# First tokens in pairs with V first, zeros on TensorE, another queue for the maxima and score tiles in fixed turn, in a fused attention and gated MLP block

## The chip, the cores and the metric

The kernel runs on one core of a Trainium2 chip. The metric is the device time of one execution in microseconds (us). The engines are called as in the profile: PE (TensorE, matrix products; PEld is its weight load), DVE (VectorE), ACT (ScalarE), POOL (GpSimd) and SP (SyncE, which issues DMA transfers). A suffix q stands for an engine's queue, where it waits or issues.

## The reference

One layer norm feeds two branches, and the results and the input are added.

```python
xn = _layernorm(x)                                   # x: 1 x 2048 x 512
qkv = (xn @ wqkv) ...                                # 32 heads of 16
p = softmax(einsum("bhqd,bhkd->bhqk", q, k) * 16 ** -0.5)
attn = einsum("bhqk,bhkd->bhqd", p, v) ... @ wo
z = gelu(xn @ w_in);  z1, z2 = halves of z           # 896 wide each
g = einsum("ts,bsf->btf", w_sp, layernorm(z2)) + b_sp
out = x + attn + (z1 * g) @ w_out
```

Everything is float32.

## The kernel before, in words

Products are made in three parts: each operand is split into a high part (a rounded copy) and a low part (the rest), and `mm3` (L161) adds high by high, low by high and high by low into one PSUM bank. `split` (L157) does this for a PSUM tile: ACT copies the high part, DVE subtracts.

**The first stage** (L816 to L854) makes normed tokens, q and k of the first eight heads, and all of V. Tokens come in four groups of 512, each of four tiles of 128. `load_x` (L223) brings two tiles a transfer. `norm_x` (L233) takes statistics on DVE, a square root on ACT, two small DVE operations, and scales the tiles on ACT. `turn_x` (L255) turns a group with 16 PE transposes, four for each block of 128 channels, splits each block and stores it for later stages through GpSimd's queue. A block takes a PSUM tile from `spsum` (L153), of which there are three of two banks. `begin` (L168) loads a weight block in full and, with `early`, loads it a second time through GpSimd's queue straight into the rounded high part; `end` (L182) then subtracts on DVE, or, without `early`, GpSimd does both steps. `qk_group` (L287) makes q and k of a group, 24 products; `v_tile` (L334) makes V of 128 tokens, 12 products, and ACT empties the bank. The order on PE is: group 0 turned, q and k of group 0, V tiles 0 and 1, group 1 turned, V tiles 2 and 3, q and k of group 1, and so on. `load_stacks` (L598) reads q and k back from DRAM into stacks with the rows laid out for the score products.

**The attention loop** (L943 to L1014) goes over 16 pairs of heads x 4 chunks of 512 queries x 16 tiles of 128 keys, 1024 steps, three steps in every two half steps. In a half step PE makes score tiles (`scores`, L898: tile st, two products) and, 27 steps ahead, tiles of raw scores with queries on the partitions (`max_mm`, L622: tile mx); both come from `spsum`. ACT exponentiates st into pf (`exp`, L920); DVE reduces mx to maxima (`max_red`, L632). `max_fin` (L640) ends 16 tiles of maxima in 64 places: five small DVE operations, the last a transpose (L657), then a store of 16 KB to the scratch mscr one half step later, and two half steps later four loads from it into the rows of the q stack that carry the negated maxima into the score products. `pv` (L864) multiplies pf by V into tile o. `later` (L125) puts a transfer off by so many half steps; `move` (L100) issues on SP's queue, `store` (L134) on GpSimd's in the first stage and on SP's after it.

Between these, a planner inserts steps of dense work (`queue`, L857): the rest of q and k, both halves of the MLP's input (`z2_all`, `z1_all`), the product over tokens (`spatial`), the MLP's output (`mlp_out`, L565, which loads its hidden tile and x one tile ahead) and the attention's output (`attn_out`). Engine order is the order of the code. Tiles of a pool with a tag share its buffers; a tile that reuses one waits for the last reader of the old content.

Of the kernel before, what the change touches and what calls it, by code (L numbers as in the profile page):

```python
# [16 lines left out]
P = 128  # L17
# [14 lines left out]
RING = 20  # L32
LEAD = 27
# [6 lines left out]
def fused_block(ctx, tc, x, wqkv, wo, w_in, w_spT, b_sp, w_out, out):  # L40
# [86 lines left out]

    def flush():
# [23 lines left out]

    def spsum(nm):  # L153

        return ps.tile([P, 2, 512], F32, tag="s", name=nm, bufs=3)
# [12 lines left out]
    def begin(nm, src, n, blocks=1, t=None, early=None):  # L168


        t = piece(nm) if t is None else t
        rw = t512(nm + "r") if early == "t" else big.tile([P, 512], F32, tag="raw", name=nm + "r", bufs=3)
        dst, hi = rw[:, :n], t[:, 0, :n]
        if blocks > 1:
            src = src.rearrange("(c p) f -> p c f", p=P)
            dst, hi = (v.rearrange("p (c f) -> p c f", c=blocks) for v in (dst, hi))
        move(dst, src)
        if early:
            nc.gpsimd.dma_start(hi, src)
        return t, rw, n  # L180

    def end(loaded, early=False):  # L182
        t, rw, n = loaded
        if early:
            nc.vector.tensor_sub(t[:, 1, :n], rw[:, :n], t[:, 0, :n].bitcast(F32))
        else:
            gps(0.6).tensor_copy(t[:, 0, :n], rw[:, :n])  # L187
            gps(1.3).tensor_sub(t[:, 1, :n], rw[:, :n], t[:, 0, :n].bitcast(F32))
        return t
# [33 lines left out]
    def load_x(g):  # L223
        xt = [at.tile([P, 2, D], F32, tag="pf", name=f"x{g}_{i}", bufs=PF) for i in (0, 2)]
        for i in range(len(xt)):
            k = 4 // len(xt)
            t = 4 * g + k * i
            rows = x[t * P:(t + k) * P, :]
            move(xt[i], rows if k == 1 else rows.rearrange("(a p) d -> p a d", p=P))
            for j in range(k):  # L230
                xs[g, k * i + j] = xt[i] if k == 1 else xt[i][:, j, :]

    def norm_x(g, parts=1):  # L233
# [5 lines left out]
        for a in range(parts):  # L239
            tiles = range(a * k, (a + 1) * k)  # L240
            sl = slice(a * k, (a + 1) * k)
            for i in tiles:
                st = sm.tile([P, 6], F32, tag="bst", name=f"bst{g}_{i}", bufs=4)
                nc.vector.bn_stats(st, xs[g, i])
# [4 lines left out]
            nc.vector.scalar_tensor_tensor(rs[:, 1, sl], mv[:, sl, 0], -1.0, rs[:, 0, sl], ALU.mult, ALU.mult)  # L249
            for i in tiles:  # L250
                if i % 4 == 2:
                    yield
                nc.scalar.activation(xs[g, i], xs[g, i], AF.Identity, bias=rs[:, 1, i:i + 1], scale=rs[:, 0, i:i + 1])

    def turn_x(g):  # L255
        for c in range(ND):
            pt = spsum(f"xT{g}_{c}")[:, 0, :]
            for i in range(4):
                nc.tensor.transpose(pt[:, i * P:(i + 1) * P], xs[g, i][:, c * P:(c + 1) * P], ident)
            t = piece(f"xnT{g}_{c}")  # L260
            split(t[:, 0, :], t[:, 1, :], pt, 512)
            store(xscr[g][c], t)
            xnT[g, c] = t
# [70 lines left out]
    def v_tile(t, ws):  # L334
        acc = dpsum(f"v{t}", "do"[t % 2])
        sl = slice((t % 4) * P, (t % 4 + 1) * P)
        for c in range(ND):
            xt = xnT[t // 4, c]
# [226 lines left out]
    def mlp_out():  # L565
        def load(t):
            hp = []
            for i, n in enumerate((4, 3)):
                h = piece(f"hp{t}_{i}")
                move(h[:, :, :n * P].rearrange("p a (f q) -> p a f q", q=P), hscr[t // 4][:, :, t % 4, 4 * i:4 * i + n, :])  # L570
                hp.append(h)
            xt = t512(f"xr{t}")
            move(xt, x[t * P:(t + 1) * P, :])
# [38 lines left out]
    NSTEP = NP * 64  # L612
    mstep = {}
# [26 lines left out]
    def max_fin(i):  # L640
# [18 lines left out]
        later(1, move, mscr[g % 4].rearrange("b k x -> (b k) x"), ms)  # L659
# [155 lines left out]
    with tc.manual_schedule(engines=engines):  # L815
        load_x(0)  # L816
        w0 = [begin(*qk_weights(0, a), early="t") for a in range(2)]
        load_x(1)
        ones = big.tile([P, 512], F32, tag="raw", name="ones", bufs=3)
        nc.vector.memset(ones[0:32, 0:P], 1.0)  # L820
        wv = []
        for c in range(ND):
            t = (qst, kst)[c // 2][1].rearrange("p (b a f) -> p b a f", b=2, a=2)[:, c % 2]
            wv.append(begin(f"wv{c}", wqkv[c * P:(c + 1) * P, 2 * D:3 * D], 512, t=t, early="rt"[c % 2]))
        nc.gpsimd.dma_start(cscr.rearrange("o (a b) -> (o a) b", b=P), ones[0:16, 0:P])
        nc.gpsimd.memset(vhead[:, :, :, DH:], 1.0)
        nc.gpsimd.memset(vall[:, NT * H * (DH + 1):], 0.0)
        run(norm_x(0, 2))
        load_x(2)
        w0 = [end(l, True) for l in w0]  # L830
        turn_x(0)
        load_x(3)
        init_rows(0)
        wv = [end(l, True) for l in wv]
        norm = norm_x(1, 2)
        for g in range(NG):
            for y in qk_group(0, g, w0, ("d", "o")):
                if y == 0 and g == 0:
                    next(norm, 0)
# [7 lines left out]
            for t in range(4 * g, 4 * g + 4):  # L847
# [95 lines left out]
        for half in range(-2 * LEAD // 3, 2 * (N // 3 + 4)):  # L943
# [25 lines left out]
            for n in ns[1:]:  # L969
                exp(n)  # L970
            for f in final:
# [81 lines left out]
```

## Time and profile before

| | |
|---|---|
| median of 3 runs | 1966.16 us (1964.69 to 1969.37) |
| profiled execution | 1965.23 us, its span 1963.1 us |
| mean granted clock of PE | 0.997 |
| DMA moved | 294.20 MB, mean 150 GB/s |
| busy share of PE in the first 10 us | 0.92 of 10.00 us |

In rows of the order of time, the first number is the start in us from the span's start, the second how long it took, then engine, line, operation, output<-inputs by the program's names, shapes and how many were merged. In brackets stands the idle time of the engine ahead of it and what ended it. In rows of stretches stand, for each engine, busy us and how many instructions, and at the end the granted clock of PE, the share of the DMA engines that was busy, and GB/s. In lists of waits stand the total in us, how often, and the longest.

### The profile page before, as it was taken

Reading aid. Unit: us, or ns where it says so; the run is one execution under the profiler, and the core shown is the slowest. Engines: PE = TensorE matmul, PEld = TensorE weight load, DVE = VectorE, ACT = ScalarE, POOL = GpSimd, SP = SyncE. Lnnn points to the kernel's source line nnn. Section 1 sums busy time; section 2 is a strip of 40 time slices with the busy share of each in tenths; the row PEclk is TensorE's granted clock in tenths of the full one; section 3 lists DMA queues with packets and bytes.
Section 4 is the critical chain, followed back from the end, with each engine's and each line's share of the span. In section 5 each row is a group of like instructions: output and inputs, shape, how many; then the busy total and the mean of one; then the engine's idle time right before and its main releaser. Section 6 shows DMA issues by size and latency. Waiting matters only on the chain.

```text
span 1963.1 us, 32545 instructions
## 1 busy us (share of the span) xinstructions
PE 1933.9 (99%) x12544; PEld 1047.0 (53%) x12544; DVE 1372.9 (70%) x1562; ACT 1231.7 (63%) x1402; POOL 720.9 (37%) x787
## 2 busy tenths in 40 slices
PE   7999999999999999999999999999999999999998
PEld 6765555555555555555555555555555555555543
DVE  5256777777777677777777777777777777777872
ACT  4336778888777665656666665665566655556664
POOL 2234368789776931026122531017112300002100
PEclk9999999999999999999999999999999999999999
DMA  9586444363535645365545744346364645355323
GB/s 327 204 292 200 139 107 122 108 176 111 154 117 159 187 123 140 91 162 159 151 138 154 211 129 125 108 126 204 105 163 135 176 142 145 106 152 154 105 73 113
DMA packets 234195, 294.20 MB, mean 150 GB/s; under 512 B 34536, under 2 KB 134520, under 8 KB 231160
## 3 DMA queue, kind: packets, MB, share of 16 engines
q1 hardware_dynamic: 229816, 282.08, 49.4%
q0 software_dynamic: 4224, 10.04, 1.4%
q8 instruction: 99, 1.62, 0.3%
q14 instruction: 56, 0.46, 0.1%
HBM read 190.09 MB, written 101.97 MB: 149 GB/s over the span
## 4 chain that ended last, share of the span: by engine, by line
PE 91%; DVE 3%; POOL 2%; DMA 2%; ACT 1%; issue 1%; SPq 0%; DVEq 0%; POOLq 0%; ACTq 0%
PE o L877 23%; PE mx L630 15%; PE st L903 15%; PE sp L162 7%; PE sp L164 5%; PE sp L163 5%; PE mo L162 2%; PE z1p L162 2%; PE qk L162 1%; DVE mm L638 1%; PE mo L163 1%; PE mo L164 1%; PE z2p L162 1%; PE z1p L164 1%; PE z1p L163 1%; PE qk L163 1%
## 5 line engine op out<-in xcount | busy, mean ns | idle before, releaser
L638 DVE TENSOR_REDUCE mm<-mx 128x2 f32<-128x1024 f32 x1024 | 1221.5, 1222 | 501.3 <-PE mx L630 497.2
L57 ACT ACTIVATE pf<-st 128x1024 f32<-128x1024 f32 x1024 | 1028.7, 1025 | 621.9 <-PE st L903 597.2
L877 PE MATMUL o<-pf,vall 128*32 128x512 f32 (+1 forms) x5120 | 511.0, 513 | 0.0
L630 PE MATMUL mx<-kst,qst 48*128 48x512 f32 x2048 | 446.9, 434 | 3.1 <-DVE mm L638 2.0
L903 PE MATMUL st<-qst,kst 50*128 50x512 f32 x2048 | 445.6, 432 | 1.5 <-DVE mm L638 1.4
L630 PEld LDWEIGHTS mx<-kst,qst 48*128 48x128 f32 x2048 | 192.0, 185 | 268.7 <-ACT pf L57 168.6
L903 PEld LDWEIGHTS st<-qst,kst 50*128 50x128 f32 x2048 | 193.3, 185 | 164.0 <-issue 85.7
L877 PEld LDWEIGHTS o<-pf,vall 128*32 128x32 f32 x5120 | 131.4, 109 | 233.7 <-issue 211.7
L162 PE MATMUL sp<-wsp,zs 128*128 128x512 f32 x448 | 193.8, 433 | 0.3 <-DVE z1i L549 0.2
L556 POOL TENSOR_TENSOR z1i<-z1i,hhl 128x512 f32<-128x512 f32 x28 | 36.0, 1286 | 425.9 <-DVE z1i L549 422.4
L164 PE MATMUL sp<-wsp,zs 128*128 128x512 f32 x448 | 175.9, 393 | 0.0
L163 PE MATMUL sp<-wsp,zs 128*128 128x512 f32 x448 | 175.9, 393 | 0.0
L162 PEld LDWEIGHTS sp<-wsp,zs 128*128 128x128 f32 x448 | 83.9, 187 | 68.9 <-issue 52.1
L164 PEld LDWEIGHTS sp<-wsp,zs 128*128 128x128 f32 x448 | 84.1, 188 | 19.3
L163 PEld LDWEIGHTS sp<-wsp,zs 128*128 128x128 f32 x448 | 84.4, 188 | 12.2
L187 POOL CAST wo<-wo0r 128x512 fp32r<-128x512 f32 x1 | 0.6, 611 | 191.4 <-DMA wo0r<-in_wo 191.4
L310 POOL TENSOR_TENSOR qkhl<-qr,qkhl 128x512 fp32r<-128x512 f32 x24 | 30.9, 1289 | 78.9 <-ACT qkhl L57 78.8
L162 PE MATMUL z2p<-w,xt 128*128 128x448 f32 x128 | 51.3, 401 | 0.0
L162 PE MATMUL mo<-wout,hp 128*128 128x512 f32 x112 | 48.5, 433 | 0.6 <-DVE xr L593 0.4
L691 POOL TENSOR_TENSOR ob<-ob 128x512 f32<-128x512 f32 (+1 forms) x16 | 20.6, 1288 | 77.0 <-DMA ob<-rscr 54.5
L164 PE MATMUL z2p<-w,xt 128*128 128x448 f32 x128 | 46.9, 366 | 0.0
L163 PE MATMUL z2p<-w,xt 128*128 128x448 f32 x128 | 46.8, 365 | 0.0
(378 smaller groups left out, 1974.8 us busy)
## 6 DMA issues: line engine op xcount, KB each, us to landing
zs<-z2scr SPq DMA_DIRECT2D x112, 512.0 KB
escr<-e SPq DMA_DIRECT2D x60, 256.0 KB
hscr<-hhl SPq DMA_DIRECT2D x28, 512.0 KB
qst<-qscr SPq DMA_DIRECT2D x30, 384.0 KB
kst<-kscr SPq DMA_DIRECT2D x30, 384.0 KB
xscr<-xnT POOLq DMA_DIRECT2D x16, 512.0 KB, 6.0
qscr<-qkhl SPq DMA_DIRECT2D x16, 512.0 KB
kscr<-qkhl SPq DMA_DIRECT2D x16, 512.0 KB
```

What stands on the lines that cost most here:

```text
L57: return nc.scalar.activation(out, in_, func, **kw)
L162: nc.tensor.matmul(acc, lh, rh, start=first, stop=False)
L163: nc.tensor.matmul(acc, ll, rh, start=False, stop=False)
L164: nc.tensor.matmul(acc, lh, rl, start=False, stop=last)
L187: gps(0.6).tensor_copy(t[:, 0, :n], rw[:, :n])
L310: gps(1.3).tensor_sub(hl[:, 1, :], src, hl[:, 0, :].bitcast(F32))
L556: gps(1.3).tensor_add(z1, z1, hl[:, 1, :].bitcast(F32))
L630: nc.tensor.matmul(acc[:, j, :], qst[p % 2][rows, tt * P:(tt + 1) * P], kst[p % 2][rows, kc * 512:(kc + 1) * 512], start=True, stop=True)
L638: dve(1024).tensor_reduce(mmax[i // 16][:, :, t, kc], mstep.pop(i), AX.X, ALU.max)
L691: gps(1.3).tensor_mul(both[rows, 0, :], both[rows, 0, :], both[rows, 2, :])
L877: nc.tensor.matmul(acc[cols:cols + VW, a:a + w], vpack(kt - 1 + r, 2 * p + j), pf[:, j * 512 + a:j * 512 + a + w], start=(kt == 1 and a == ...
L903: nc.tensor.matmul(st[:, j, :], kst[p % 2][rows, kt * P:(kt + 1) * P], qst[p % 2][rows, c * 512:(c + 1) * 512], start=True, stop=True)
```

## The change

- **First stage.** Group 0's tiles are loaded one by one: two, then V's four weight blocks, then the other two, then the weights of q and k, then groups 1 and 2. All early loads go through SP's queue; the second loads through GpSimd's are gone. GpSimd casts V's high parts; DVE subtracts three of the low parts and GpSimd the fourth; GpSimd makes both parts of the q and k weights. Group 0 is normed and turned in pairs of tiles: the first pair, V tiles 0 and 1, the second pair, V tiles 2 and 3, then q; group 1 is turned between q and k of group 0. Group 1 is normed in pairs too, between V tiles 2 and 3.
- `turn_x` takes three PSUM tiles of two banks at once, makes all transposes, and then splits.
- 15 products of zeros (`WARM`) stand first on PE. Their operand is set by DVE. A square root on ACT stands first there.
- `spsum` gives the three tiles strictly in turn.
- The store of maxima leaves SP's queue for ACT's: it is kept in `behind` and issued behind the exponentials of a half step.
- In `mlp_out` the loads for all tiles but the first are put off by 1, 2 and 3 half steps.

```diff
@@ spsum
-        return ps.tile([P, 2, 512], F32, tag="s", name=nm, bufs=3)
+        turns[0] += 1
+        return ps.tile([P, 2, 512], F32, tag=f"s{turns[0] % 3}", name=nm, bufs=1)
@@ begin, end
-        if early:
-            nc.gpsimd.dma_start(hi, src)
...
-    def end(loaded, early=False):
+    def end(loaded, low=None, high=False):
         t, rw, n = loaded
-        if early:
-            nc.vector.tensor_sub(t[:, 1, :n], rw[:, :n], t[:, 0, :n].bitcast(F32))
+        if high:
+            low.tensor_sub(t[:, 1, :n], rw[:, :n], t[:, 0, :n].bitcast(F32))
...
@@ turn_x
+    def turn_x(g, lo=0, hi=4):
+        tiles = [spsum(f"xT{g}_{lo}_{c}") for c in range(3)]
+        sl = slice(lo * P, hi * P)
+        for c in range(ND):
+            for i in range(lo, hi):
+                nc.tensor.transpose(tiles[c % 3][:, c // 3, i * P:(i + 1) * P], xs[g, i][:, c * P:(c + 1) * P], ident)
+        for c in range(ND):
+            if lo == 0:
+                xnT[g, c] = piece(f"xnT{g}_{c}")
+            t = xnT[g, c]
+            split(t[:, 0, sl], t[:, 1, sl], tiles[c % 3][:, c // 3, sl], (hi - lo) * P)
+            if hi == 4:
+                store(xscr[g][c], t)
@@ mlp_out
-                move(h[:, :, :n * P]..., hscr[...])
+                (later if t else soon)(i + 1, move, h[:, :, :n * P]..., hscr[...])
...
-            move(xt, x[t * P:(t + 1) * P, :])
+            (later if t else soon)(3, move, xt, x[t * P:(t + 1) * P, :])
@@ max_fin and the loop
-        later(1, move, mscr[g % 4].rearrange("b k x -> (b k) x"), ms)
+        behind.append((now[0] + 1, mscr[g % 4].rearrange("b k x -> (b k) x"), ms))
...
             for n in ns[1:]:
                 exp(n)
+            while behind and behind[0][0] <= half:
+                nc.scalar.dma_start(*behind.pop(0)[1:])
@@ first stage
+        nc.scalar.activation(mhalf, epst, AF.Sqrt)
+        idle = piece("idle")
+        nc.vector.memset(idle.bitcast(F32)[:, 0, :], 0.0)
+        nc.vector.memset(mhalf, -0.5)
+        rest = dpsum("idle", "o")
+        for _ in range(WARM):
+            nc.tensor.matmul(rest, idle[:, 0, 0:P], idle[:, 0, :], start=True, stop=True)
...
+        for t, rw, n in wv:
+            nc.gpsimd.tensor_copy(t[:, 0, :], rw)
+        norm = norm_x(0, 2)
+        next(norm)
+        next(norm)
+        wv = [end(l, (nc.vector, nc.gpsimd)[c == 3], True) for c, l in enumerate(wv)]
+        turn_x(0, 0, 2)
+        next(norm)
...
+        w0 = [end(l) for l in w0]
+        run(norm)
+        v_tile(0, wv)
+        v_tile(1, wv)
+        turn_x(0, 2, 4)
+        norm1 = norm_x(1, 2)
+        next(norm1)
+        v_tile(2, wv)
+        next(norm1)
+        next(norm1)
+        v_tile(3, wv)
+        run(norm1)
```

More of the change, by code (lines that the diff above doesn't have):

```diff
@@ L32 @@
 RING = 20
+WARM = 15
 LEAD = 27
@@ L126, in later, with soon @@
         late.append((now[0] + k, fn, args))
+    def soon(k, fn, *args):
+        fn(*args)
     def flush():
@@ L337, in v_tile @@
         for c in range(ND):
+            if c == 2 and mid:
+                mid(t + 1)
             xt = xnT[t // 4, c]
@@ L612, in fused_block @@
     NSTEP = NP * 64
+    behind = []
     mstep = {}
@@ L815, in fused_block @@
     with tc.manual_schedule(engines=engines):
[L816 to L820, printed above, removed]
+        nc.scalar.activation(mhalf, epst, AF.Sqrt)
[5 more added lines that the diff above has]
+            nc.tensor.matmul(rest, idle[:, 0, 0:P], idle[:, 0, :], start=True, stop=True)
+        first = load_x(0)
+        next(first)
+        next(first)
         wv = []
@@ L824, in fused_block @@
             wv.append(begin(f"wv{c}", wqkv[c * P:(c + 1) * P, 2 * D:3 * D], 512, t=t, early="rt"[c % 2]))
+        run(first)
+        w0 = [begin(*qk_weights(0, a), early="t") for a in range(2)]
+        run(load_x(1))
+        run(load_x(2))
+        ones = big.tile([P, 512], F32, tag="raw", name="ones", bufs=3)
+        nc.vector.memset(ones[0:32, 0:P], 1.0)
+        for t, rw, n in wv:
[6 more added lines that the diff above has]
+        next(norm)
         nc.gpsimd.dma_start(cscr.rearrange("o (a b) -> (o a) b", b=P), ones[0:16, 0:P])
@@ L846, in fused_block @@
                     wq[1, a] = end(wq[1, a])
-            for t in range(4 * g, 4 * g + 4):
+            for t in range(4 * g, 4 * g + 4) if g else ():
                 next(norm, 0)
```

53 lines of the change are left out of this document (28 added, 25 removed).

## The prediction, made before the changed kernel ran

> **What bounds the kernel now.** I read the page first, then the stretches (busy time by window), then the order of time of the first 35 us and of 130 to 150 us, and last the idle rows of TensorE (the list of waits).
>
> ```profile
> span 1963.1 us, 32545 instructions
> PE 1933.9 (99%) x12544; PEld 1047.0 (53%) x12544; DVE 1372.9 (70%) x1562; ACT 1231.7 (63%) x1402; POOL 720.9 (37%) x787
> ```
>
> TensorE bounds the whole: busy for 1933.9 of 1963.1 us. All its idle time together is 29 us, so no change that leaves TensorE's instructions alone can gain more than 1.5%. The change leaves them alone from the first score tile on: in the two programs TensorE and VectorE have the same sequence of instructions in the attention loop. What can move is the 29 us of idle time and the time in which TensorE runs at a lower clock. About a third of the idle time lies ahead of 13.6 us:
>
> ```profile
> 0.73 0.96 SPq L101 DMA_DIRECT2D x<-in_x  x2
> 4.54 0.69 DVE L244 BATCH_NORM_STATS2 bst<-x 128x6 f32<-128x512 f32 x1 [3.46 <-DMA x<-in_x]
> 7.01 1.52 ACT L253 ACTIVATE x<-x,rs 128x512 f32<-128x512 f32 x2 [0.43 <-DVE rs L249]
> 7.92 0.45 PE L259 MATMUL xT<-ident,x 128*128 128x128 f32 x1 [7.92 <-ACT x L253]
> 9.34 1.52 ACT L253 ACTIVATE x<-x,rs 128x512 f32<-128x512 f32 x2 [0.43 <-DVE rs L249]
> 10.91 3.04 PE L259 MATMUL xT<-ident,x 128*128 128x128 f32 x13 [0.23 <-ACT x L253]
> 11.43 0.60 ACT L57 ACTIVATE xnT<-xT 128x512 fp32r<-128x512 f32 x1 [0.57 <-PE xT L259]
> 12.06 0.69 DVE L159 TENSOR_TENSOR xnT<-xT,xnT 128x512 fp32r<-128x512 f32 x1
> 13.60 0.63 PE L162 MATMUL qk<-xnT,wqk 128*128 128x512 f32 x1
> 14.07 0.39 PE L163 MATMUL qk<-xnT,wqk 128*128 128x512 f32 x1
> 14.30 0.39 PE L164 MATMUL qk<-xnT,wqk 128*128 128x512 f32 x1
> ```
>
> The chain is load, statistics, scaling (two pairs, one after the other, then all four tiles are needed), 16 transposes, split, first product at 13.60. The first product starts 0.47 us ahead of the second, the second 0.23 ahead of the third: TensorE goes from half to full clock at about 14.0, and 0.227 us is the pitch of a product from there on. After that it idles little, in two places that the change touches. The last column of the rows below is the idle time and what ended it:
>
> ```profile
> 25.80 1.20 PE L259 MATMUL xT<-ident,x 128*128 128x128 f32 x9 [0.28 <-ACT x L253]
> 27.54 0.66 PE L259 MATMUL xT<-ident,x 128*128 128x128 f32 x4 [0.54 <-DVE xnT L159]
> 33.50 0.39 PE L162 MATMUL qk<-xnT,wqk 128*128 128x512 f32 x1
> 46.45 0.66 PE L259 MATMUL xT<-ident,x 128*128 128x128 f32 x4 [0.59 <-DVE xnT L159]
> 65.38 0.66 PE L259 MATMUL xT<-ident,x 128*128 128x128 f32 x4 [0.59 <-DVE xnT L159]
> 135.00:140.00 5.00, 3.45 (x15) 2.36 (x14) 1.23 (x1) 2.24 (x5) 2.51 (x2) 1.00 0.96 369
> 137.35 0.50 PE L162 MATMUL qk<-xnT__1182,wqk 128*128 128x512 f32 x1 [1.55 <-ACT qr L57]
> 144.50 1.94 ACT L57 ACTIVATE pf<-st 128x1024 f32<-128x1024 f32 x2 [0.61 <-PE st L903]
> 146.00 0.50 PE L630 MATMUL mx<-kst,qst 48*128 48x512 f32 x2 [1.08 <-DVE mm L638]
> 147.96 0.63 PE L164 MATMUL qk<-xnT__1182,wqk 128*128 128x512 f32 x1
> 147.00:148.00 1.00, 1.00 (x3) 0.81 (x4) 1.00 (x2) 0.99 (x2) 0.28 (x1) 0.53 0.59 223
> 150.00:151.00 1.00, 1.00 (x9) 0.54 (x9) 0.13 (x1) 0.37 (x1) 0.00 (x0) 0.76 1.03 387
> ```
>
> In the three stretches, the third number from the end is the granted clock: full around 137, 0.53 in the us from 147, 0.76 in the one from 150. In between, products take 0.63 us instead of 0.39; shares of 0.53 and 0.76 put the half clock from 147.1 to 150.5.
>
> **The change, part by part.**
>
> *First tokens by pairs, V first.* Added at the front: one load per 128 tokens, V's weights behind the first two of these, and GpSimd's casts of all six blocks. Removed: six loads that GpSimd issued for the weights' high parts (1.5 MB that are now made on chip). The first 0.25 MB tile should land no later than the 0.5 MB pair did (4.54), and not before half of its way, 0.73 + 3.8/2 = 2.6. I take 4.0 for the first tile and 4.54 for the second, so that statistics end some 0.5 us sooner. With that, scaling runs from 6.5 to 8.0 (1.52). The first copy began 0.52 us after its last transpose (10.91 to 11.43): 8.55. A copy of half the width took 0.38:
>
> ```profile
> 1951.26 0.38 ACT L57 ACTIVATE e<-o 128x256 f32<-128x256 f32 x1 [2.42 <-PE o L877]
> 87.52 0.61 POOL L187 CAST wqk<-wqk_0r 128x512 fp32r<-128x512 f32 x1 [15.38 <-DMA wqk_0r<-in_wqkv]
> 88.22 1.29 POOL L188 TENSOR_TENSOR wqk<-wqk_0r,wqk 128x512 fp32r<-128x512 f32 x1
> 33.70 0.60 ACT L57 ACTIVATE vall<-v 128x512 f32<-128x512 f32 x1 [2.12 <-PE v L164]
> ```
>
> So V's first product can start at 9.0 in place of 13.60. Its weights: GpSimd casts four blocks (0.61 each, 2.4 in all) as they land; the three subtractions on VectorE (0.6 pitch, from 6.5) stand ahead of the first subtraction of xnT and end at 8.3, before it is due at 9.0. GpSimd's own subtraction (1.29) is due with V's last block, 2 us later. Cover: 0.7 us; if a weight block lands 1 us later than I think, 0.3 us of it shows.
>
> Then I follow the new order. The second product waits for VectorE's half-width subtraction (0.4), then 11 pitches of 0.227: v0 ends at 12.0, v1 at 14.7. The second pair's statistics stand on VectorE behind four half subtractions (to 10.6), take 1.7, then 0.8 for the factors, scaling 13.1 to 14.6. ScalarE then empties v0 and v1 (0.60 each) ahead of the second pair's copies: TensorE has transposed by 15.7 and waits until 16.3, and 0.4 more for VectorE. v2 and v3 end at 22.0, the first q product group at 24.7; the third pair is scaled by 25.0 (two rounds of 0.60 + 0.3 + 0.4 + 1.5 behind v2 and v3), 0.3 us of idle time; 16 transposes and the k group end at 29.2. The same work (72 products, 32 transposes) was over at 33.50: **4.3 us ahead**. Two more groups of transposes follow, with all four blocks in three tiles of two banks, so that the fourth no longer waits for a release: 0.59 twice. **Together 5.5 us.** End to end these bounds: 6.8 if tile 0 lands at 2.6 and statistics are a full 1.5 sooner with it; 2.5 if tile loads gain nothing (0.5), ScalarE's order costs two evacuations more (1.2), and TensorE runs 3.4 us at half clock in V (1.5). GpSimd's splits of the q and k weights (2 x 1.9) end near 15, used from 22.0.
>
> *Products of zeros.* Fifteen of them, at the cold pitch of 0.43 (row 147.96 stands 0.43 ahead of the next), start at about 1.4 and end between 6.4 and 7.9, ahead of the first transposes at 7.3. If late they delay those by 0.5 at most. They are worth the cold transposes (13 in 3.04 us at 10.91, 9 in 1.20 at 25.80), mostly off the path that I have priced already; I count nothing, and they hold up nothing else, for TensorE has no other work.
>
> But the clock can fall again. An idle time of 1.08 us ahead of 146.00 was followed by those 3.4 us at half clock, while 1.55 us ahead of 137.35 was not. Between the zeros and V lies 0.1 to 1.4 us of idle time. Eight products at 0.43 in place of 0.227 are 1.6 us: a rival below. [...]
>
> *Score tiles in turn.* In the program of before 12 tiles reuse the one two places back instead of three. One of those shows in the trace: the maxima tile at 146.00 waited for VectorE's maxima of the tile before it. In turn it waits for the first exponential (144.50, two in 1.94), so to about 145.55: 0.4 us gained. The half-clock stretch behind it may go too (1.6 us); since one like it may arise at V, I count neither. The other eleven show no wait; elsewhere nothing changes. Bounds 0 to 2.7.
>
> *Maxima by own queue.* 64 stores of 16 KB leave SyncE's queue for ScalarE's.
>
> ```profile
> SPq L101 <- DVE ms L657: 210.8, 58, 15.4
> SPq L101 <- DMA mscr<-ms: 81.1, 48, 6.4
> L101 SPq DMA_DIRECT2D mscr<-ms x64: 314/326/627, 117.0 to 1907.9; - x64
> 727.02 0.21 DVE L657 STREAM_TRANSPOSE ms<-mrow 128x32 f32<-128x32 f32 x1
> 727.53 1.02 ACT L57 ACTIVATE pf<-st 128x1024 f32<-128x1024 f32 x1 [0.63 <-PE st L903]
> 729.78 2.06 ACT L57 ACTIVATE pf<-st 128x1024 f32<-128x1024 f32 x2 [1.22 <-PE st L903]
> 732.09 0.40 PE L630 MATMUL mx<-kst,qst 48*128 48x512 f32 x2
> 1883.00 2.16 ACT L57 ACTIVATE pf<-st 128x1024 f32<-128x1024 f32 x2 [0.56 <-PE st L903]
> 1.29 1.00 POOL L179 DMA_DIRECT2D wqk<-in_wqkv  x1 [0.36 <-issue]
> 1796.88 1.84 SPq L101 DMA_DIRECT2D op<-oscr  x3
> 1801.21 0.32 SPq L101 DMA_DIRECT2D mscr<-ms  x1
> ```
>
> SyncE waited 210.8 us for these maxima, and what stood behind waited along; but the loads of them back stay on SyncE and wait for the store, so most of that wait only moves, and TensorE waits for no transfer in the loop. I count nothing. On ScalarE the store stands behind the third exponential of a step: maxima ready at 727.23, exponential over at 728.55, next one at 729.78. No wait for the data, and 1.22 us free for an issue that took SyncE 0.33. I went through the 63 such places that the loop has: the maxima are ready before the exponential ends in all, and the least free time is 0.56 us (ahead of 1883.00). Behind the store on ScalarE stand the next exponentials, and TensorE waits for those. It also shares a semaphore with the transfer eight places ahead; the nearest of those was issued 4.3 us before (1796.88, against 1801.21), time enough to land. Bounds: 0 by SyncE's row; the unknown issue time on ScalarE is the slow rival. At 117 us the store leaves as early as before, so the queue jam that ends in the 1.55 us at 137.35 stays: the loads of maxima hold SyncE just as long.
>
> *The output stage's loads* go 1 to 3 half steps later, and are asked for a whole tile ahead. The code plans 880 steps of dense work over 931 score steps, three of which are two half steps: 1.4 in each half step, so a tile of seven fills 5. The first blocks, one half step late, keep 4 half steps (11 us at the code's 2.7) to land. Counted at nothing; if that cover were gone, a wait of 1 or 2 us at some of 16 tiles.
>
> **Sum.** 5.5 + 0.4 = 5.9 us off 1965.23 (the profiled execution: span 1963.1 and 2.1 around it) is 1959.3. The runs' median, 1966.16, lies 0.9 above the profiled one; I go half way: **1959.8 us**.
>
> **Rivals.**
> 1. *More goes*: the half-clock stretch after 146.00 does not come back anywhere, and Q's store, freed of its wait, eases the jam ahead of 137.35. 1.6 + up to 1.5 more: 1956.7. For: the shorter idle time. Against: the loads of maxima still block SyncE.
> 2. *Half clock at V*: 1.6 us back, 1961.4. For: the row at 146.00. Counted with the forecast.
> 3. *The start is given back*: ScalarE is the single server of scaling, copies and evacuations, and TensorE waits for it between the pairs; or V's weights come late in the one queue. Lead 1 to 2.5 us, 1963 to 1965: the change doesn't do what it says. For: ScalarE's order puts evacuations ahead of copies. Against: its work to 25 us sums to some 15 us (eight scalings of 0.76, eight half copies of 0.38, four evacuations of 0.60, four roots of 0.3, a table).
> 4. *Slower*: ScalarE is held x us by each of the 64 stores. Free are 1.2 us in the usual place, and TensorE reaches the next tile 0.25 us later (exponentials over at 731.84, the tile that needs it at 732.09), so the loop loses 64 (x - 1.5). Level with the gain of 5.9 at x = 1.6; at x = 1.8 the loss is 19, 1979. For: ScalarE has never issued one here, and one of GpSimd's took 1.00 us. Against: SyncE's 0.33.
>
> **How the numbers follow.** Forecast with rival 2: 0.60 (1957.5 to 1962.2, a little of it above). Rival 1: 0.15. Rival 3: 0.14. Rival 4 and its kin: 0.11. About 0.2% (3.9 us) is what a measurement of this kernel can tell from no change; 1966.2 - 3.9 = 1962.3. Faster 0.60 - 0.03 + 0.15 = 0.72, same 0.03 + 0.14 = 0.17, slower 0.11. The range goes from 1955.5 (rival 1 and the 0.9 that I halved) to 1965.0 (rival 3).
>
> **What would show it.** V's first product near 9 and the k group's end near 29.2; no idle time of 0.5 ahead of the transposes after that; first maxima some 5.5 us sooner; the maxima tile after the first exponentials idle for 0.65 in place of 1.08; the 1.55 still there; issues on ScalarE near 0.33 with no new idle time ahead of score tiles. Wrong it would be if TensorE's idle time in the loop grows, or if V starts after 11.

## The result, and the profile after

The changed kernel takes **1960.54 us** (median of 8 runs, 1959.0 to 1963.75), the kernel before 1965.74 beside it on the same chip (8 runs, 1964.69 to 1969.64). The ratio is 0.9973, 95% interval 0.9964 to 0.9983: faster by 0.27%. The profiled executions are 1965.23 us before and 1960.41 after; the rest compares these two.

First the page of the changed kernel, then rows in order of time: the first statistics on VectorE, and TensorE up to the first maxima tile.

```profile
span 1958.6 us, 32589 instructions
PE 1937.7 (99%) x12559; PEld 1049.6 (54%) x12559; DVE 1374.3 (70%) x1565; ACT 1232.3 (63%) x1407; POOL 725.3 (37%) x790
```

```profile
3.42 0.69 DVE L259 BATCH_NORM_STATS2 bst<-x 128x6 f32<-128x512 f32 x1 [0.94 <-DMA x<-in_x]
1.54 6.37 PE L845 MATMUL idle<-idle 128*128 128x512 f32 x15 [1.54 <-DVE idle L841]
7.75 1.12 PE L276 MATMUL xT<-ident,x 128*128 128x128 f32 x8
9.43 0.47 PE L170 MATMUL v<-qst,xnT 128*128 128x512 f32 x1 [0.57 <-ACT xnT L58]
9.96 0.50 PE L171 MATMUL v<-qst,xnT 128*128 128x512 f32 x1
17.39 0.51 PE L170 MATMUL v<-qst,xnT 128*128 128x512 f32 x1 [0.47 <-ACT xnT L58]
30.43 0.39 PE L170 MATMUL qk<-xnT,wqk 128*128 128x512 f32 x1
42.27 0.98 PE L276 MATMUL xT<-ident,x 128*128 128x128 f32 x7 [0.37 <-ACT x L268]
83.72 0.50 PE L653 MATMUL mx<-kst,qst 48*128 48x512 f32 x2
```

TensorE's first real product stands at 9.43 instead of 13.60. The 73rd product (behind 72 products and 32 transposes) starts at 30.43 instead of 33.50, and the first maxima tile, which had stood here:

```profile
87.76 0.50 PE L630 MATMUL mx<-kst,qst 48*128 48x512 f32 x2
```

now stands at 83.72: **4.04 us ahead**. From there to the last eight products the two programs take 1867.10 and 1866.65 us (worked out from their start at 1954.86 and 1950.37), so nearly the whole gain is made ahead of the loop. The places at 137.35 and 146.00 have come through, 4 us earlier. In the rows of stretches the granted clock is the third number from the end:

```profile
133.29 0.50 PE L170 MATMUL qk<-xnT__1211,wqk 128*128 128x512 f32 x1 [1.52 <-ACT qr L58]
139.40 1.28 ACT L58 ACT_TABLE_LOAD   x1
140.69 1.94 ACT L58 ACTIVATE pf<-st 128x1024 f32<-128x1024 f32 x2
141.77 0.50 PE L653 MATMUL mx<-kst,qst 48*128 48x512 f32 x2 [0.95 <-ACT pf L58]
142.68 0.50 PE L653 MATMUL mx<-kst,qst 48*128 48x512 f32 x2 [0.18 <-ACT pf L58]
140.40:143.81 3.41, 2.29 (x13) 1.06 (x10) 2.72 (x3) 3.32 (x6) 0.34 (x1) 1.00 0.98 364
143.81:147.23 3.42, 3.42 (x15) 1.83 (x17) 1.32 (x2) 1.82 (x3) 1.28 (x1) 0.50 0.34 127
```

The jam stayed (1.52), the wait behind it is now for the first exponentials, as the prediction said, but 0.95 + 0.18 long, and the half clock came back for 3.42 us. SyncE's waits for the maxima moved from the data to the store, and ScalarE issues the stores as fast as SyncE did:

```profile
SPq L102 <- DMA mscr<-ms: 301.3, 60, 16.2
L1027 ACTq DMA_DIRECT2D mscr<-ms x64: 326/326/359, 113.0 to 1903.6; - x64
```

Before, it was 210.8 for the data and 81.1 for the store, 291.9 together.

### The profile page after: what moved, and what is told of

It reads as the page before. It is cut to its first block, busy times and chain, and to the rows that moved or that the text cites. A ratio compares the mean times of both kernels' runs of the same rounds, so it can differ in the third digit from the quotient of the medians.

```text
span 1958.6 us, 32589 instructions
## 1 busy us (share of the span) xinstructions
PE 1937.7 (99%) x12559; PEld 1049.6 (54%) x12559; DVE 1374.3 (70%) x1565; ACT 1232.3 (63%) x1407; POOL 725.3 (37%) x790
## 3 DMA queue, kind: packets, MB, share of 16 engines
q10 hardware_dynamic: 9216, 1.05, 0.4%
## 4 chain that ended last, share of the span: by engine, by line
PE 86%; POOL 3%; DVE 2%; ACT 1%; issue 1%; DMA 0%; DVEq 0%; POOLq 0%; ACTq 0%
PE o L932 23%; PE st L958 15%; PE mx L653 15%; PE sp L170 7%; PE sp L172 5%; PE sp L171 5%; PE mo L170 2%; PE z1p L170 2%; PE mo L171 1%; PE mo L172 1%; PE z1p L172 1%; PE z1p L171 1%; PE z2p L170 1%; DVE mm L661 1%; PE ao L170 1%; PE z2p L172 1%
```

## The experiments

Eleven kernels stand in three groups, each beside the kernel before, run again on the same chip (medians 1965.69, 1965.06 and 1965.50). Single runs of one kernel lie 1.5 to 6.7 us apart, once 8, so each effect is looked for in the trace as well. Of the parts of the first stage, the zeros and the new turning were run alone; the loads by tile, the pairs and V first were not, so what these are worth is read from rows only. In the table "first maxima" is the start of the first maxima tile, "idle" is TensorE's from 120 to 150 us, and "half" says whether a stretch at half clock followed between 136 and 152; all three are of the profiled execution.

| kernel | median us | ratio, 95% interval | first maxima | idle | half |
|---|---|---|---|---|---|
| before | 1965.74 | | 87.76 | 2.63 | yes |
| changed | 1960.54 | 0.9964 to 0.9983 | 83.72 | 2.64 | yes |
| one zero product | 1961.86 | 0.9966 to 0.9984 | 85.15 | 2.78 | yes |
| store on SyncE | 1961.79 | 0.9969 to 0.9987 | 84.26 | 3.36 | yes |
| tiles as free | 1960.29 | 0.9955 to 0.9980 | 83.92 | 2.43 | no |
| GpSimd's order | 1959.86 | 0.9958 to 0.9981 | 83.34 | 2.43 | no |
| before + new turning | 1963.87 | 0.9984 to 1.0002 | 88.20 | 2.15 | no |
| before + zeros | 1966.11 | 0.9995 to 1.0012 | 88.61 | 2.43 | no |
| before + zeros between | 1966.93 | 0.9994 to 1.0012 | 87.73 | 2.96 | yes |
| V tile 1 emptied later | 1960.18 | 0.9962 to 0.9983 | 83.35 | 2.33 | yes |
| loads of maxima later | 1959.87 | 0.9962 to 0.9983 | 83.78 | 0.67 | no |
| output loads at once | 1958.94 | 0.9955 to 0.9980 | 83.42 | 2.52 | no |
| GpSimd's order + first loads later | **1957.18** | 0.9945 to 0.9970 | 83.78 | 0.67 | no |

**One zero product.** The theory under test is the prediction's, that the zeros are worth nothing.

```diff
-WARM = 15
+WARM = 1
```

> The changed kernel with 1 product of zeros in place of 15, nothing else. The prediction counted nothing for the zeros: then the time stays within 1 us of the changed kernel's 1960.5 us, and the lead at the first maxima tile (83.72 in the changed kernel's trace) stays within 0.5. [...]

Its start on TensorE, in order of time, and two stretches:

```profile
7.41 1.76 PE L276 MATMUL xT<-ident,x 128*128 128x128 f32 x7 [0.17 <-ACT x L268]
9.73 0.77 PE L170 MATMUL v<-qst,xnT 128*128 128x512 f32 x1 [0.56 <-ACT xnT L58]
10.25:13.67 3.42, 3.42 (x9) 2.55 (x9) 2.95 (x10) 0.68 (x2) 3.33 (x6) 1.00 1.07 376
13.67:17.08 3.41, 3.41 (x17) 2.79 (x16) 1.12 (x1) 2.00 (x3) 2.96 (x3) 1.00 1.03 379
```

In 3.4 us TensorE starts 9 products, in the next 3.4 us 17: it is cold (at half clock) until 13.67, though the profile prints a granted clock of 1.00 ahead of its first record of a change. V tile 2 starts at 18.81 instead of 17.39, the first maxima tile 1.43 us later than in the changed kernel. But V's weights landed late in this execution: GpSimd's first cast starts at 6.13, in the changed kernel at 5.65. In the run with the store on SyncE (below) it starts at 6.20, and there the first maxima tile stands at 84.26, 0.89 sooner than here. So the zeros are worth 0.9 to 1.4 us. The medians, 1.3 us apart, have intervals that overlap.

**The store on SyncE** undoes the change of queue alone, **tiles as free** the fixed turn of score tiles.

```diff
-        behind.append((now[0] + 1, mscr[g % 4].rearrange("b k x -> (b k) x"), ms))
+        later(1, move, mscr[g % 4].rearrange("b k x -> (b k) x"), ms)
```

> The changed kernel with the 64 stores of maxima issued by SyncE again, as before the change. My theory: the queue of these stores is worth nothing either way (ScalarE's issues took 0.326 us each and the free time there was 0.56 or more), so 1960.5 within 1 us and the same list of TensorE idle places from 90 us on. Rival A, the stores cost ScalarE time that shows: faster by up to 64 x 0.33, some 20 us at most, at least 2. Rival B, the move helps by freeing SyncE: slower by 2 us or more, and the idle time ahead of 133.29 (1.52) grows.

```diff
-        return ps.tile([P, 2, 512], F32, tag=f"s{turns[0] % 3}", name=nm, bufs=1)
+        return ps.tile([P, 2, 512], F32, tag="s", name=nm, bufs=3)
```

> The changed kernel with the score tiles handed out as they come free again (one tag with three buffers), the transposes still three tiles at once. My theory: only the tile at 141.77 (idle 0.95 in the changed kernel) can differ, by 0.2, and the single wait of 0.33 that stood at 474.40 before may come back: 1960.5 to 1961.5. Rival: fixed turns shape the whole loop, then the idle time of TensorE between 200 and 1900 us (2.4 us in both traces) would change by more than 1, and the time by more than 1.5 us.

The queue: 1961.79 against 1960.54, a little outside the range expected, with intervals that overlap in the main. Of the profiled execution's 2.3 us, 0.54 are there at the first maxima tile already (V's second product waits 0.81 us for VectorE), and 0.72 more idle time arises at the jam, 3.36 us in all, where the kernel before with the same queue had 2.63; of the remaining 1 us, 0.55 is in the last eight products, which run at half clock here (last section), and the rest is not assigned. The wait that ends at the jam is 1.78 us here, but it is 1.76 to 1.80 in three runs with the store on ScalarE too (one zero product, GpSimd's order, output loads at once). No cost or gain of the queue itself is shown. The 64 issues on ScalarE cost TensorE nothing that shows: its idle time from 150 to 1877 us is 2.95 us in the changed kernel and 2.82 with the store on SyncE. The turn: here the tile behind the jam waits for VectorE's maxima again, and in the run with the output loads at once, which has the turn, for the exponentials (one row of each):

```profile
141.82 0.50 PE L653 MATMUL mx<-kst,qst 48*128 48x512 f32 x2 [1.08 <-DVE mm L661]
```

```profile
141.85 0.49 PE L653 MATMUL mx<-kst,qst 48*128 48x512 f32 x2 [0.67 <-ACT pf L58]
```

The difference is 0.41 us. Of the eight kernels with the turn five show 0.67 there, the others 0.88, 0.95 and 1.58. It is too small for the medians (1960.29 against 1960.54). In the profiled execution of the changed kernel itself, ScalarE's table load (139.40 to 140.69, above) ended late, behind a wait of 1.63 us for a store of q, and took most of it away.

**GpSimd's order.** In the changed kernel VectorE's smallest operation lasts 0.59 and 1.24 us instead of the 0.16 it took in the kernel before, each time beside an instruction of GpSimd. The second does so in all six executions with this order of GpSimd (1.23 to 1.27), the first in this one and, with 0.27, in one more. Rows of both engines in order of time:

```profile
5.65 0.61 POOL L860 CAST qst<-wv0r 128x512 fp32r<-128x512 f32 x1 [4.35 <-DMA wv0r<-in_wqkv]
5.68 0.59 DVE L264 SCALAR_TENSOR_TENSOR rs<-mv,rs 128x2 f32<-128x2 f32 x1
7.49 1.07 DVE L191 TENSOR_TENSOR qst<-wv1r,qst 128x512 fp32r<-128x512 f32 x1 [0.51 <-POOL qst L860]
7.96 1.07 POOL L860 CAST kst<-wv3r 128x512 fp32r<-128x512 f32 x1
8.48 1.09 DVE L191 TENSOR_TENSOR kst<-wv2r,kst 128x512 fp32r<-128x512 f32 x1
13.03 1.28 POOL L197 TENSOR_TENSOR wqk<-wqk_0r,wqk 128x512 fp32r<-128x512 f32 x1
13.08 1.24 DVE L264 SCALAR_TENSOR_TENSOR rs<-mv,rs 128x2 f32<-128x2 f32 x1
```

The small operation starts 0.03 and 0.05 us behind GpSimd's and ends with it, 0.01 us later. The experiment moves GpSimd's preparation of V's tile and its store of constants ahead of its casts, which shifts all of GpSimd's later work.

```diff
+        nc.gpsimd.dma_start(cscr.rearrange("o (a b) -> (o a) b", b=P), ones[0:16, 0:P])
+        nc.gpsimd.memset(vhead[:, :, :, DH:], 1.0)
+        nc.gpsimd.memset(vall[:, NT * H * (DH + 1):], 0.0)
         for t, rw, n in wv:
             nc.gpsimd.tensor_copy(t[:, 0, :], rw)
...
         next(norm)
-        nc.gpsimd.dma_start(cscr.rearrange("o (a b) -> (o a) b", b=P), ones[0:16, 0:P])
-        nc.gpsimd.memset(vhead[:, :, :, DH:], 1.0)
-        nc.gpsimd.memset(vall[:, NT * H * (DH + 1):], 0.0)
```

> The changed kernel with GpSimd's two sets of ones and zeros in V's tile and its small store moved ahead of its casts of V's weights, where it idles from 1.3 to 5.65. No work is added. Theory: VectorE's small product of factors at 13.08 took 1.24 us in place of 0.16 because it could not begin while GpSimd subtracted (13.03 to 14.31); with GpSimd's four splits of the q and k weights 1.2 to 1.4 us sooner that product takes 0.2 to 0.5, the second pair is scaled 0.8 to 1.1 sooner, V tile 2 starts at 16.5 to 16.9 in place of 17.39 and the time falls by 0.4 to 0.9, to 1959.6 to 1960.1. Rival: the product is slow for a reason of its own; then it takes 1.24 again and nothing moves.

```profile
5.74 0.16 DVE L264 SCALAR_TENSOR_TENSOR rs<-mv,rs 128x2 f32<-128x2 f32 x1
7.70 1.07 DVE L191 TENSOR_TENSOR qst<-wv1r,qst 128x512 fp32r<-128x512 f32 x1 [0.51 <-POOL qst L863]
8.70 1.09 DVE L191 TENSOR_TENSOR kst<-wv2r,kst 128x512 fp32r<-128x512 f32 x1
13.29 0.16 DVE L264 SCALAR_TENSOR_TENSOR rs<-mv,rs 128x2 f32<-128x2 f32 x1
10.18 0.50 PE L171 MATMUL v<-qst,xnT 128*128 128x512 f32 x1 [0.65 <-DVE xnT L167]
17.04 0.50 PE L170 MATMUL v<-qst,xnT 128*128 128x512 f32 x1 [0.47 <-ACT xnT L58]
```

The small operations are back to 0.16, in all three executions with the new order. V tile 2 stands 0.35 us sooner and the first maxima tile 0.38; no more, because the subtractions of V's weights still last 1.07 and 1.09 beside GpSimd's casts (0.69 alone), and V's second product now waits 0.65 us for the subtraction behind them. The first maxima tile alone would not prove a gain: it stands at 83.34 to 83.78 with the new order and at 83.42 to 84.26 in the five executions with 15 zeros and the old one. It moves with V's second product, which starts at 9.72 to 10.55, behind the landing of V's weights. Counted from that product, V tile 2 comes after 6.83 to 6.90 us with the new order and after 7.43 to 7.45 with the old one, so the order is worth 0.5 to 0.6 us. That the engines hold each other up is shown by both ends: in this run GpSimd's casts take 0.61 us at 5.86 and 7.61, but 1.02 and 1.07 at 6.65 and 8.17, where a subtraction of VectorE has begun already (at 6.51 and 7.70). The statistics at 11.85 in this run, which read one operand, are not held up: they take 0.66 us, though GpSimd subtracts from 11.56 on for 1.28, and 0.66 at 7.71 in the kernel before, where GpSimd is idle.

**V tile 1 emptied later** adds to that a ScalarE queue in which the emptying of V tile 1 stands behind the second pair's copies.

```diff
-        act(vhead[:, t, :, :DH], acc.rearrange("p (h d) -> p h d", d=DH), AF.Copy, 512)
+        empty = lambda: act(vhead[:, t, :, :DH], acc.rearrange("p (h d) -> p h d", d=DH), AF.Copy, 512)
+        empty() if hold is None else hold.append(empty)
...
-        v_tile(1, wv)
+        held = []
+        v_tile(1, wv, hold=held)
         turn_x(0, 2, 4)
+        held.pop()()
```

> The changed kernel with GpSimd's preparation of V's tile and its store of constants ahead of its casts, and ScalarE's emptying of V tile 1 behind the copies of the second pair. Theory (ScalarE as the single server between the pairs: 0.60 us of emptying stands ahead of the copies for which TensorE waits): V tile 2 starts 0.3 to 0.6 us ahead of 17.04, the first maxima tile 0.3 to 0.6 ahead of 83.34, time about 1959.5. Rival (VectorE's half-width subtractions set that wait, ScalarE is ahead of them anyway): V tile 2 within 0.15 us of 17.04, nothing gained.

V tile 2 stands at 16.96, 0.08 us sooner, with the same 0.47 of idle time ahead of it. On ScalarE:

```profile
16.53 1.26 ACT L58 ACTIVATE xnT<-xT 128x256 fp32r<-128x256 f32 x4 [1.09 <-PE xT L276]
```

ScalarE had been free for 1.09 us and waited for the transposes. The theory fell: the 0.47 is the first copy itself.

**The parts alone in the kernel before.** New turning, with no other edit:

```diff
+        tiles = [spsum(f"xT{g}_{c}") for c in range(3)]
         for c in range(ND):
-            pt = spsum(f"xT{g}_{c}")[:, 0, :]
             for i in range(4):
-                nc.tensor.transpose(pt[:, i * P:(i + 1) * P], ...)
+                nc.tensor.transpose(tiles[c % 3][:, c // 3, i * P:(i + 1) * P], ...)
+        for c in range(ND):
```

> The kernel before, with only the new way of turning groups of tokens: three PSUM tiles of two banks taken at once, all 16 transposes first, then the four splits. My theory (that the three waits of 0.54, 0.59 and 0.59 us ahead of the fourth block's transposes in groups 1 to 3 are what this part was worth): first maxima tile 1.2 to 1.7 us ahead of 87.76, time 1.0 to 1.7 us under the kernel before (about 1964). Rival (the transposes only move ahead of copies that then come late, so TensorE waits for the last split in place of the third): first maxima tile within 0.4 us of 87.76, time as before.

Both were right, in different groups. Behind the 73rd product (35.59) the waits are gone: 52.61 us to the first maxima tile instead of 54.26. But in group 0 the copies do come late:

```profile
14.98 0.79 PE L162 MATMUL qk<-xnT,wqk 128*128 128x512 f32 x1 [0.69 <-ACT xnT L57]
15.57 0.63 PE L163 MATMUL qk<-xnT,wqk 128*128 128x512 f32 x1
```

and products stay at the cold 0.63 until 20.01, in place of 13.95. With tokens that landed 0.34 us later than in the kernel before, the first maxima tile is 0.44 behind. The time, 1.2 us under that of before, can't be told from no change.

**Zeros alone**, and then **zeros between** the first transposes too:

```diff
+        idle = piece("idle")
+        nc.vector.memset(idle.bitcast(F32)[:, 0, :], 0.0)
+        rest = dpsum("idle", "o")
+        for _ in range(15):
+            nc.tensor.matmul(rest, idle[:, 0, 0:P], idle[:, 0, :], start=True, stop=True)
```

> The kernel before, with only the 15 products of zeros ahead of it. My theory after the run with a single product of zeros (zeros bring full clock to the first transposes and products, worth 1.4 us there): the 13 transposes in 3.04 us take about 2.2, the first product stands near 12.8 in place of 13.60 and the first maxima tile 0.8 to 1.4 us ahead of 87.76; time 0.8 to 1.4 us under the kernel before. Rival (the prediction's: the cold transposes are off the path, ScalarE's copies set it): first product within 0.3 us of 13.60, nothing gained.

```profile
6.33:9.74 3.41, 1.77 (x7) 0.84 (x5) 2.51 (x10) 2.11 (x4) 0.60 (x2) 1.00 1.37 316
9.74:13.16 3.42, 2.13 (x9) 1.85 (x10) 1.98 (x4) 2.41 (x4) 0.00 (x0) 0.50 1.16 380
13.16:16.57 3.41, 3.41 (x13) 2.82 (x12) 2.84 (x5) 1.50 (x3) 2.02 (x4) 0.50 1.13 386
```

TensorE (first pair of numbers behind the length) is busy for 1.77 us in the stretch at full clock from 6.33, and the clock is halved; 2.13 in the next, and it stays half; 3.41 in the third, and it is full again at 16.57, 2.6 us later than without zeros (13.95). My theory for this run fell: the zeros, with a wait behind them, gained nothing. The first maxima tile is 0.85 us behind the kernel before; 0.58 of that are tokens that landed later (first statistics at 5.12 instead of 4.54). The next kernel keeps TensorE busy through it.

```diff
-        for _ in range(15):
+        for _ in range(19):
...
                 nc.tensor.transpose(pt[:, i * P:(i + 1) * P], ...)
+                if g == 0 and c == 0:
+                    for _ in range((1, 5, 1, 0)[i]):
+                        nc.tensor.matmul(rest, idle[:, 0, 0:P], idle[:, 0, :], start=True, stop=True)
```

> The kernel before, with 19 products of zeros ahead and 7 more behind the first three transposes of group 0, so that TensorE is hardly idle until its first real products. Theory (the run with 15 zeros alone had full clock from 6.33 and lost it at 9.74, because TensorE was idle for 1.03, 0.36 and 1.30 us in that stretch; the zeros are only worth something when real work follows without such gaps): full clock from 6 to 8 us on without a half-clock stretch behind it, the 13 transposes in about 2.2 us, the first real product 0.4 to 0.8 us sooner than in the run with 15 zeros when compared from the landing of the first tokens, first maxima tile 0.8 to 1.5 us ahead of that run's 88.61; time 1964 to 1965. Rival (transposes do not hold the clock, whatever stands between them): half clock returns for 3.4 us or more ahead of 17, nothing gained.

```profile
7.80:11.21 3.41, 2.86 (x12) 1.70 (x13) 1.72 (x6) 2.57 (x5) 0.00 (x0) 1.00 1.23 354
13.10 0.47 PE L162 MATMUL qk<-xnT,wqk 128*128 128x512 f32 x1
19.41 0.51 PE L162 MATMUL v<-qst,xnT 128*128 128x512 f32 x1 [0.58 <-DVE qkhl L316]
```

The clock holds from 4.39 on and the first product stands at 13.10, 0.5 us sooner with tokens at the same time (4.57 against 4.54). But V's first product then waits 0.58 us for a bank that VectorE reads, and the first maxima tile is where it was (87.73). The clock half of the theory held, its gain didn't: in the old order the next wait takes it.

**Loads of maxima later** asks whether the jam is SyncE's queue or the transfers' bandwidth.

```diff
-                later(2, move, qst[p % 2][row:row + 1, ...], mscr[g % 4]...)
+                later(4, move, qst[p % 2][row:row + 1, ...], mscr[g % 4]...)
```

> The changed kernel, with the four loads of each tile of maxima put off by 4 half steps in place of 2. Theory (SyncE's queue is held because those loads wait in it for the store of the maxima, 301 us in all; what stands behind them, the fetches and stores of the dense work, is late, and this ends in the idle time of 1.5 us ahead of 133.29 and 0.95 ahead of 141.77): the wait of SyncE for mscr falls from 301 us to under 60, the idle time ahead of 133.29 falls under 0.5 us, the 3.4 us at half clock behind 143.8 go, time 1956.5 to 1959. Rival (that idle time comes from the transfers' own bandwidth, 2 MB of normed tokens in that stretch): the wait for mscr falls all the same, the idle time stays between 1.2 and 1.8 us, time within 1 us of 1960.5.

SyncE's queue (SPq), first in the changed kernel, then here; start and length of issue. The last row of the first block is ScalarE's, the last of the second TensorE's:

```profile
114.45 2.78 SPq L102 DMA_DIRECT2D qst<-mscr  x4
119.95 1.14 SPq L102 DMA_DIRECT2D xnT__1211<-xscr  x1
132.13 0.63 ACT L58 ACTIVATE qkhl<-qr 128x512 fp32r<-128x512 f32 x1 [7.13 <-DMA kscr<-qkhl]
```

```profile
114.17 0.79 SPq L102 DMA_DIRECT2D xnT__1207<-xscr  x1
1855.47 0.50 PE L653 MATMUL mx<-kst,qst 48*128 48x512 f32 x2 [1.35 <-ACT pf L58]
```

In the changed kernel the loads of maxima wait 7.3 us for their store ahead of 114.45 and hold back the normed tokens; here the same fetch (its first block is xnT__1211 there and xnT__1207 here) is issued 5.8 us earlier. What TensorE then waits for is not the tokens: it is ScalarE (133.29 above), which has waited 7.13 us for a store of k to land. The DMA engines were busy for 0.02 of the time from 110 to 115 us and 0.37 from 115 to 120, and then for 0.97 to 1.05 of it up to 135, with the tokens and these stores at once; here it is 0.62, 0.97, 1.03 and 0.99 up to 130, and then 0.54. So the rival, bandwidth, has a share in the jam, but it is SyncE's queue that crowds the transfers together. The idle time ahead of 133 is gone, and with it the half clock; the wait for the store fell to 114.8 us in all, not under 60. By 317 us the kernel is 3.0 us ahead of the changed one, against 0.06 behind at the first maxima tile. It gives 2.2 of that back between 1821 and 1877, above all in a new wait of 1.35 us at 1855.47, where exponentials come late in a stretch with the DMA engines 0.94 to 0.98 busy. So the median, 1959.87, moves by 0.7 us only and misses the range expected.

**Output loads at once** undoes the last part:

```diff
-                (later if t else soon)(i + 1, move, h[:, :, :n * P]..., hscr[...])
+                soon(i + 1, move, h[:, :, :n * P]..., hscr[...])
...
-            (later if t else soon)(3, move, xt, x[t * P:(t + 1) * P, :])
+            soon(3, move, xt, x[t * P:(t + 1) * P, :])
```

> The changed kernel, with the output stage's loads issued at once as in the kernel before. Theory (they are hidden in both ways, a whole tile ahead): TensorE's idle time between 1300 and 1900 us stays as it is, time within 0.8 us of the changed kernel's (1959.7 to 1961.3). Rival (loads put off save a jam on SyncE that holds the maxima or the normed tokens): new idle time of 1 us or more between 1500 and 1900, time 1 to 2 us longer.

No new idle time between 1300 and 1900; 1958.94 us. The interval overlaps with the changed kernel's, and its profiled execution (1958.87) has no half-clock stretch, which alone cost the changed kernel 1.3 us (last section). These loads are worth nothing that shows, in either way.

**The combination**: GpSimd's order, and `later(4 if g < 8 else 2, ...)` for the loads of maxima, so that only the first eight groups wait longer.

> The changed kernel, with GpSimd's constants ahead of its casts, and the loads of maxima put off by 4 half steps for the first eight groups of maxima alone (by 2 as before for the other 56). Theory (the early fetch of normed tokens takes the jam away, worth 1.5 us of idle time ahead of 133 and with it the half clock behind it; late loads cost 1.4 us near 1855 only because the last groups were put off too): the idle time ahead of about 133 under 0.3 us, none of 1.35 near 1855, time 1956.3 to 1957.8. Rival (the idle time at 1855 comes from transfers elsewhere, or the gained time is lost at another wait): 1959 or more.

**1957.18 us** (1956.99 to 1958.46, 5 runs), 0.43% under the kernel before (interval 0.30 to 0.55); its slowest run is under the changed kernel's fastest (1959.0). The new wait at 1855 is gone, and at the jam only the wait for the first exponentials is left (first row):

```profile
139.96 0.49 PE L653 MATMUL mx<-kst,qst 48*128 48x512 f32 x2 [0.67 <-ACT pf L58]
10.55 0.50 PE L171 MATMUL v<-qst,xnT 128*128 128x512 f32 x1 [1.08 <-DVE xnT L167]
```

The second row shows what this execution still loses at the start: V's weights landed late (GpSimd's first cast at 6.23), and their subtractions run beside the casts as before. So its first maxima tile (83.78) is no sooner than the changed kernel's, and GpSimd's order adds nothing that this profile shows. Its lead over the changed kernel's, 3.1 us at 150 us, comes from the jam and the half clock behind it.

## Why the prediction was right, and where it was not

- **The start, 5.5 us: the mechanism held, the size was 4.04** (3.50 to 4.34 in the five profiled executions with this start). The tokens were better than taken (first statistics at 3.42 instead of 4.0), but V's first product came at 9.43 instead of 9.0 and V tile 2 at 17.39 instead of 16.3. That is 1.09 of the missing 1.46 us. Two terms were mis-sized, both on VectorE beside GpSimd, since each engine was priced from rows in which the other was still. "The three subtractions on VectorE ... end at 8.3": they ended at 9.57, and V tile 1 was done at 15.3 instead of 14.7. "0.8 for the factors": it took 1.84, from 12.52 to 14.36, and the second pair was scaled that much later. GpSimd's order removed the second; the first was seen in its rows but not removed. Another 0.14 is lost up to the 73rd product. The last 0.23 is the turning of groups 2 and 3, which gave 0.97 where some 1.2 stood. Without its wait a turning is 0.80 us shorter (44.39 to 46.86 before, 60.10 to 61.77 in the changed kernel), more than the 0.59 counted; but group 2 has a new wait of 0.37 at 42.27, for ScalarE's scaling, which the prediction did not look for and which takes 0.59 of it back (41.41 to 43.67). The new turning alone, without that wait, gave 1.65.
- **Zeros, "I count nothing": wrong as a statement, harmless in the sum.** The sum let V's products run at a pitch of 0.227 from the second on, and that is what the zeros buy: 0.9 to 1.4 us, near the 1.6 that stood as the price of "half clock at V". That rival did not happen, in any of the eight profiled executions with the new order and 15 zeros. The zeros have this worth because V follows them closely; alone they had none.
- **The turn of score tiles, 0.4:** its size is shown (1.08 to 0.67), but not in the profiled execution of the changed kernel. The half-clock stretch that I counted neither way came back there, and stayed away in others.
- **The queue of maxima, 0:** right. The rival "slower" is refuted by 0.326 us for each issue on ScalarE. "Most of that wait only moves": 291.9 became 301.3 us.
- **The jam stays:** right, 1.52 for 1.55. The loads that hold SyncE were named as its reason, and putting them off removed it. That the DMA engines then have to carry everything at once, and that ScalarE waits for a store of k, the prediction did not say.
- **Output loads, 0:** nothing contrary was found.
- **Rival 1** (more goes) needed the jam to ease, which the change did not do; its 1956.7 is about what the combination reached. **Rival 3** (start given back, by ScalarE) named the wrong engine for the wait between the pairs: emptying V tile 1 later gained 0.08. Its other half, V's weights late in the one queue, did cost something in some executions: the store on SyncE and the combination lost some 0.5 us that way.

## What to carry to other kernels

Price an operation beside its neighbours: the subtractions of V's weights, with two operands, took VectorE 1.07 and 1.09 us beside GpSimd's casts, and 0.69 in the rows of an undisturbed stretch. Products of zeros paid 0.9 to 1.4 us here where real work followed closely and nothing where gaps did, and an engine freed early pays only as far as the next wait (0.5 us at the first product of the run with zeros between, none at its first maxima tile); the trace at the next milestone, not at the first product, tells what an edit was worth. When a queue holds a wait, look for what stands behind it, and put the waiting transfer off only where there is room: moved for all 64 groups it gave back 2.2 of its 3.0 us, for the first eight it kept them.

## What the runs showed of the hardware

- **The clock changed in steps of 3.41 us**, counted from its own changes (in the kernel before it is full from 13.95 to 147.07, 39 steps of 3.413, in the changed kernel from 7.28 to 143.81, 40 steps, then half for one in both). Stretches of one step can so be laid over the rows. In the score stage behind the jam, a step with 1.05 to 1.58 us of idle time (1.08 in the kernel before, from 143.66, and 1.12 in the changed one, from 140.40) was followed by half clock in five of six executions, and one with 1.00 or less in none of seven. Where products of 128 rows run, ahead of it, it is not so plain; these are steps of the runs with output loads at once and with one zero product:

```profile
131.88:135.29 3.41, 1.64 (x7) 1.38 (x8) 1.23 (x1) 1.99 (x4) 1.44 (x2) 1.00 0.88 335
```

```profile
133.14:136.55 3.41, 1.64 (x8) 0.87 (x7) 1.23 (x1) 1.11 (x2) 1.12 (x1) 1.00 0.96 371
136.55:139.97 3.42, 3.42 (x10) 2.67 (x9) 0.00 (x0) 1.75 (x3) 2.12 (x3) 0.50 0.74 276
```

TensorE is busy for 1.64 us in both first rows; the one kernel kept full clock up to 1951, the other lost it in the next step. What is counted in a step stays open.
- A stretch at half clock cost 1.3 us in the changed kernel: from the product at 143.17 to the one at 149.02 it takes 5.85 us, and the run with output loads at once, at full clock, takes 4.56 for the same instructions (143.26 to 147.82). Whether a stretch falls behind the jam differs between the profiled executions. The same holds at the end: ahead of the last eight products TensorE waits 2.03 us for VectorE in every execution, and these products take 1.14 us in six of the 13 and 1.63 to 2.09 in the other seven, where the clock has halved ahead of them or among them (at 1947.55 in the combination, 1.98 us). Both may be part of why runs of one kernel lie up to 8 us apart; the combination, without the jam, spreads over 1.5 us only in five runs, but the run with the loads of maxima later, without it too, over 2.4 in seven. Runs without a profile don't show it.
